# A fused attention and SwiGLU kernel: a POOL chain put first, a centring step one batch later, and Down products spread between Gate and Up pairs

## The chip, the core and the metric

The kernel runs on one core of a Trainium2 chip. The metric is the device time of one execution in microseconds (us). The engines have the profile's names: PE (TensorE, matmul), PEld (its weight loads), DVE (VectorE), ACT (ScalarE), POOL (GpSimd) and SP (SyncE, which only issues DMAs here).

## The reference, cut to what matters

```python
x = A_x                                   # 1 x 2048 x 512, float32
xn = layernorm(x)                         # per token: (x - mean) / sqrt(var + 1e-5)
q, k, v = split(xn @ A_wqkv)              # 32 heads of 16
p = softmax(mask(q @ k.T * 16**-0.5))     # causal, window of 256 keys
s = (p @ v) @ A_wo
h = silu(xn @ B_w1) * (xn @ B_w3)         # Gate and Up: 512 -> 1792
g = silu(h @ B_w2)                        # Down: 1792 -> 512
out = x + s * g
```

## The kernel before, in words

**Tiles.** The 2048 tokens are four tiles `t` of 512, and each tile has four blocks `b` of 128. A float32 product is made from float16 pairs: an operand is cut into a high and a low half, and three matmuls (high·high, high·low, low·high) replace one. So a Gate or an Up product of one 128-wide slice `f` of the 1792 features is 12 matmuls of 128x512 (L1032), issued in two halves of 6. The slices are 0 to 13; `gate_up(t, f)` gives four pieces: Gate's two halves, Up's two halves. PE writes them to one of two PSUM banks, m0 and m1, which every dense product takes in turn (`bank`). ACT then makes tanh of Gate (L1047), DVE multiplies it with Gate's bank (L1051) and later with Up's bank (L1056), and ACT and POOL cut the result into halves (L1065, L339).

**Down products.** For tiles 0 and 1, `down(t, k, b)` multiplies one block of tokens with one group `k` of feature slices: groups are slices 0–3, 4–7, 8–10 and 11–13 (`GROUPS`). With four slices that is 12 matmuls (L1257) in two pieces; DVE takes the bank out (L1278 for the first group, L1281 for the others). Tiles 2 and 3 use a folded form of Down (`folds`, L1175) instead.

**Weights in tile 0.** The Gate, Up and Down weights come in as float32 and are measured and cut beside the other work while tile 0 runs: `measure` (squares on ACT, L249), a short DVE chain for the scale (L294 to L304), and `cut` by `split_pool`: ACT scales (L342), ACT casts the high half (L343), and POOL subtracts for the low half in two pieces of 256 columns (L339). Down's weights go the same way (`measure_down`, L919, L923 to L941). The cut halves are stored to DRAM and only loaded again for the later tiles.

**Token statistics.** `prepare(t)` loads a tile's x, makes mean and variance on DVE (`stats`, L437 and L438), the reciprocal root (`rstd`), and subtracts and scales (`centre`, L475 on DVE). For t > 0 `rstd` starts with three small DVE instructions (L442, L446, L447) and goes on with ten POOL instructions of 128x4 that depend on one another (L463 to L472); their result `rs` is what `centre` waits for. `prepare_beside` puts these steps into a list, and one entry of it is issued with each batch of attention work: for tiles 2 and 3 four `stats`, `rstd`, four `centre`, and then the transposes (`turn_beside`) on PE.

**Order of the work.** Attention work is issued in batches (`batches`, `spread`): score products for the maxima (L661; the maxima on DVE at L675), score products for the softmax (L742; DVE adds the mask, L749; ACT makes the exponential, L752), and the products with V (L770). Between the batches stand the dense pieces in the order of the list that `feed_forward` returns, together with the projections (L593, emptied at L610 and L614) and the V product (L563). A counter goes up by one with each dense piece and each batch; `later(n, f)` runs `f` n steps after now. PE's instructions run in the order in which they are written. The other engines' queues are ordered by a scheduler, by priority; `urgent()` raises the priority of what stands inside. All engines take their queues strictly in order. SBUF tiles of one size ("slots") are given out from a pool of 54 and taken back in order of age.

**The Down list.** In `feed_forward` the variable `late` holds pieces that are appended after the next slice's Gate and Up pieces. When the last slice of a group has been done, all four blocks of `down` go into `late`, and so stand as one lump of up to 48 matmuls behind the next Gate/Up pair.

Of the kernel before, what the change touches and what calls it, by code (L numbers as in the profile page):

```python
# [15 lines left out]
ALU = mybir.AluOpType  # L16
# [18 lines left out]
FB = F // P  # L35
# [4 lines left out]
XS = 2.0**10  # L40
# [14 lines left out]
GROUPS = ((0, 4), (4, 8), (8, 11), (11, 14))  # L55
# [28 lines left out]
def tile_block(ctx: ExitStack, tc: tile.TileContext, x, wqkv, wo, w1, w3, w2, out):  # L84
# [53 lines left out]
    def urgent():  # L138


        return tc.high_priority(offset=200) if started else nullcontext()
# [21 lines left out]
    def bank(shape, dtype=F32):  # L163

        open_bank[0] = b = 1 - open_bank[0]
        return psm.tile(shape, dtype, name=f"m{b}", tag=f"m{b}", bufs=1)
# [258 lines left out]
    def prepare(t):  # L425

        mv = lnpool.tile([P, 4, 2], F32, name="mv")
        rs = lnpool.tile([P, 4], F32, name="rs")
        xts = {}

        def load(b):
            xts[b] = take(F32)
            (nc.scalar if t == 0 and b % 2 else nc.sync).dma_start(xts[b], x[t * TW + b * P:t * TW + (b + 1) * P, :])

        def stats(b):
            st = lnpool.tile([P, nc.vector.BN_STATS_DIM], F32, name="st")
            nc.vector.bn_stats(st, xts[b])  # L437
            nc.vector.bn_aggr(mv[:, b, :], st)  # L438

        def rstd(b0, b1):  # L440
            ve = lnpool.tile([P, b1 - b0], F32, name="ve")
            nc.vector.tensor_scalar(ve, mv[:, b0:b1, 1], 1e-5, None, op0=ALU.add)  # L442


            r0 = lnpool.tile([P, b1 - b0], F32, name="r0")
            nc.vector.tensor_scalar(r0.bitcast(I32), ve.bitcast(I32), 1, None, op0=ALU.logical_shift_right)  # L446
            nc.vector.tensor_scalar(r0.bitcast(I32), r0.bitcast(I32), -1.0, float(0x5F3759DF), op0=ALU.mult, op1=ALU.add)  # L447
            sq = lnpool.tile([P, b1 - b0], F32, name="sq")
            if t == 0:
                nc.vector.tensor_mul(sq, r0, r0)  # L450
                nc.vector.tensor_mul(sq, sq, ve)

                nc.vector.scalar_tensor_tensor(sq, sq, -10 / 3, sq, op0=ALU.add, op1=ALU.mult)
                nc.vector.scalar_tensor_tensor(r0, sq, 5.0, r0, op0=ALU.add, op1=ALU.mult)
                with tc.issue_after(lasts["cast"].ins):
                    nc.vector.tensor_mul(sq, r0, r0)
                nc.vector.scalar_tensor_tensor(sq, sq, -0.5 * (3 / 8)**3 * XS, ve, op0=ALU.mult, op1=ALU.mult)
                nc.vector.scalar_tensor_tensor(rs[:, b0:b1], sq, 1.5 * (3 / 8) * XS, r0, op0=ALU.add, op1=ALU.mult)
                return

            pool = nc.gpsimd
            u = lnpool.tile([P, b1 - b0], F32, name="u")
            pool.tensor_mul(sq, r0, r0)  # L463
            pool.tensor_mul(sq, sq, ve)
            pool.tensor_scalar(u, sq, -10 / 3, None, op0=ALU.add)
            pool.tensor_mul(sq, sq, u)
            pool.tensor_scalar(sq, sq, 5.0, None, op0=ALU.add)
            pool.tensor_mul(r0, r0, sq)
            pool.tensor_mul(sq, r0, r0)
            pool.tensor_mul(sq, sq, ve)  # L470
            pool.tensor_scalar(sq, sq, -0.5 * (3 / 8)**3 * XS, 1.5 * (3 / 8) * XS, op0=ALU.mult, op1=ALU.add)
            pool.tensor_mul(rs[:, b0:b1], sq, r0)  # L472

        def centre(b):
            lasts["centre"] = nc.vector.tensor_scalar(xts[b], xts[b], mv[:, b, 0:1], rs[:, b:b + 1],  # L475
                                                      op0=ALU.subtract, op1=ALU.mult)

        def turn(b):
            if t not in X:
                X[t] = xpool.tile([P, NC, TW], F16, name="XH"), xpool.tile([P, NC, TW], F16, name="XL")  # L480
            xh, xl = X[t]
            c = slice(b * P, (b + 1) * P)

            if b < 2:
                pt = bank([P, NC, P])
            elif b == 2:
                pt = pso.tile([P, 2, TW], F32, name="po")[:, 0, :].rearrange("p (k q) -> p k q", q=P)
            else:
                pt = scores_bank()[:, 0, :].rearrange("p (k q) -> p k q", q=P)
            for k in range(NC):  # L490
                nc.tensor.transpose(pt[:, k, :], xts[b][:, k * P:(k + 1) * P], identf)
            give(xts.pop(b))
            with urgent():
                lasts["xh"] = nc.scalar.copy(xh[:, :, c], pt)

            def rest():
                turned[t] = turned.get(t, 0) + 1
                with urgent():
                    lasts["x"] = nc.vector.tensor_sub(xl[:, :, c], pt, xh[:, :, c])
            later(1, rest)  # L500

        def turn_beside(b, n, s):


            if t not in X:
                X[t] = xpool.tile([P, NC, TW], F16, name="XH"), xpool.tile([P, NC, TW], F16, name="XL")
            xh, xl = X[t]
            for k in range(n, n + 2):
                for h in range(2):
                    for c in range(2):  # L510
                        f = k * P + 64 * c
                        rows = slice(64 * h, 64 * h + 64)
                        nc.tensor.matmul(s[64 * c:64 * c + 64, h, WIN + 64 * (k - n):WIN + 64 * (k - n + 1)],  # L513
                                         xts[b][rows, f:f + 64], identf[rows, rows], start=True, stop=True)
            if n:
                give(xts.pop(b))

            def rest():
                pt = s[:, :, WIN:WIN + P].rearrange("p h (k q) -> p k h q", k=2)
                hi, lo = (a[:, n:n + 2, b * P:(b + 1) * P].rearrange("p k (h q) -> p k h q", h=2) for a in (xh, xl))  # L520
                with urgent():
                    nc.vector.tensor_copy(hi, pt)
                    nc.vector.tensor_sub(lo, pt, hi)
                if n:
                    turned[t] = turned.get(t, 0) + 1
            return rest
        return load, stats, rstd, centre, turn if t == 0 else turn_beside

    def prepare_beside(t, more=0):


        load, stats, rstd, centre, turn = prepare(t)
        made = [(0, lambda b=b: load(b)) for b in range(4)]
        pairs = [(0, 1), (2, 3)] if t == 1 else [(b,) for b in range(4)]
        work = [lambda bs=bs: [stats(b) for b in bs] for bs in pairs]
        work.append(lambda: rstd(0, 4))
        work += [lambda bs=bs: [centre(b) for b in bs] for bs in pairs]
        ready = []

        def turns():  # L540

            ready.append(0)
            if len(ready) == 2:
                besides.extend(lambda s, b=b, n=n: turn(b, n, s) for b in range(4) for n in (0, 2))
        work.append(turns)
        made.append((0, lambda: later(more, lambda: behind.extend(work))))
        return made, turns
# [684 lines left out]
    def folds(t, k):  # L1232

        loads = [(0, lambda kind=kind: load_fold(t, k, kind)) for kind in range(len(KINDS))]
        pieces = []
        for n, i in enumerate(SEVEN):
            pieces += fold_down_piece(t, k, i)
            if n in (0, 2):
                pieces.append(loads[2 + n // 2])
        return loads[:2], pieces  # L1240
# [110 lines left out]
    def feed_forward():  # L1351

        pieces = []
        late = []
        cuts_at = []
        for t in range(NT):
            for f in range(FB):
                if t == 0:
# [8 lines left out]
                    for m in range(f + 1 if f else 0, min(f + 2, FB)):  # L1367
                        k = next(k for k, (_, f1) in enumerate(GROUPS) if m < f1)
                        pieces.append((0, lambda k=k, m=m: later(2, lambda: measure_down(k, m))))
                else:  # L1370
# [7 lines left out]
                    if t == 1 and f in FOLD_AT:  # L1378
                        work = fold_weights(FOLD_AT.index(f))
# [12 lines left out]
                    if t == 1 and f == at:  # L1392
                        made.insert(2, (0, lambda work=work: later(6, work[2])))
                pieces += made
                pieces += late
                late = []
                if t < 2:
                    for k, (f0, f1) in enumerate(GROUPS):
                        if f == f1 - 1:
                            late = [q for b in range(4) for q in down(t, k, b)]  # L1400
                for k, (j0, j1) in enumerate(FOLDS):
                    if t > 1 and f == 2 * j1 - 1:
                        soon, late = folds(t, k)
                        if k == 0 or t == NT - 1:
                            pieces += soon
            if t + 2 < NT:
                pieces.append((0, second))
        return pieces + late


    tiles = [(t, g) for t in range(NT) for g in range(NG)]
# [190 lines left out]
    for n in range(len(units)):  # L1602
        t = n // 8
# [8 lines left out]
        b = n % 8 - (2 if t < 3 else 3)  # L1612
# [6 lines left out]
    for n, u in enumerate(units):  # L1619
# [17 lines left out]
        k = n // 2 + 2  # L1637
# [35 lines left out]
```

## Time and profile before

| | |
|---|---|
| median of 3 runs | 818.14 us (816.59 to 819.52) |
| the profiled execution's own time | 817.82 us |
| its span, first to last instruction | 816.0 us |
| PE busy | 795.2 us, 97% of the span |
| DVE busy | 633.9 us, 78% |
| ACT busy | 392.4 us, 48% |
| POOL busy | 364.0 us, 45% |

The span is 1.82 us shorter than the execution's own time, and that part is not in the trace. A row of the timeline gives the start in us from the span's start, the length of the merged row, the engine, line, operation, tiles and shapes, how many instructions were merged, and in brackets how long the engine was idle just before and whose result ended that. A merged row's length runs from the first start to the last end. PE's matmuls are pipelined: one 128x512 matmul shows about 380 ns, while the next one starts 216 ns after it.

### The profile page before, as it was taken

Reading aid. Unit: us, or ns where it says so; the run is one execution under the profiler, and the core shown is the slowest. Engines: PE = TensorE matmul, PEld = TensorE weight load, DVE = VectorE, ACT = ScalarE, POOL = GpSimd, SP = SyncE. Lnnn points to the kernel's source line nnn. Section 1 sums busy time; section 2 is a strip of 40 time slices with the busy share of each in tenths; the row PEclk is TensorE's granted clock in tenths of the full one; section 3 lists DMA queues with packets and bytes.
Section 4 is the critical chain, followed back from the end, with each engine's and each line's share of the span. In section 5 each row is a group of like instructions: output and inputs, shape, how many; then the busy total and the mean of one; then the engine's idle time right before and its main releaser. Section 6 shows DMA issues by size and latency. Waiting matters only on the chain.

```text
span 816.0 us, 23868 instructions
## 1 busy us (share of the span) xinstructions
PE 795.2 (97%) x9176; PEld 404.2 (50%) x9176; DVE 633.9 (78%) x2037; ACT 392.4 (48%) x591; POOL 364.0 (45%) x648
## 2 busy tenths in 40 slices
PE   8999989998999999999999999999999999999998
PEld 4434444443444444444444544456544654466465
DVE  8788788885898777787988888786777887775437
ACT  6879586563527444444444344434444334344421
POOL 2234266232328636434445264630246377560670
PEclk9999999999999999999999999999999999999999
DMA  9967554735457384666755544646362545325321
GB/s 284 258 218 254 165 179 130 276 115 188 136 141 255 105 267 120 215 180 208 204 169 171 172 100 144 168 128 189 122 197 74 161 127 149 111 77 181 111 56 70
DMA packets 109794, 134.18 MB, mean 164 GB/s; under 512 B 18864, under 2 KB 64880, under 8 KB 109680
## 3 DMA queue, kind: packets, MB, share of 16 engines
q1 hardware_dynamic: 109392, 132.13, 53.9%
q8 instruction: 72, 1.18, 0.6%
q10 hardware_dynamic: 288, 0.52, 0.2%
q14 instruction: 42, 0.34, 0.1%
HBM read 91.23 MB, written 36.57 MB: 157 GB/s over the span
## 4 chain that ended last, share of the span: by engine, by line
PE 78%; DVE 10%; ACT 5%; DMA 3%; issue 3%; SPq 1%; POOL 1%; DVEq 0%; POOLq 0%; ACTq 0%
PE m L1032 29%; PE po L770 8%; PE m L1257 8%; PE m L1175 8%; PE m L593 7%; PE s L742 5%; PE m L1309 4%; PE m L563 4%; PE s L661 3%; DVE junk L675 2%; PE po L661 2%; DMA slot<-in_A_x_dram 1%; DMA dW<-slot 1%; DVE s L749 1%; ACT slot L342 1%
## 5 line engine op out<-in xcount | busy, mean ns | idle before, releaser
L1032 PE MATMUL m<-XH,slot 128*128 128x512 f16 x896 | 267.5, 380 | 1.8 <-DVE slot L614 1.2
L752 ACT ACTIVATE pt<-s,es 128x1024 f32<-128x1024 f32 x152 | 167.6, 1112 | 198.6 <-DVE s L749 183.1
L339 POOL TENSOR_TENSOR slot<-slot,slot 128x256 f16<-128x256 f32 (+1 forms) x170 | 112.9, 691 | 218.2 <-ACT slot L1065 79.2
L1032 PEld LDWEIGHTS <-slot 128*128 128x128 f16 x1344 | 124.8, 98 | 156.2 <-issue 12.7
L1032 PE MATMUL m<-XL,slot 128*128 128x512 f16 x448 | 169.9, 379 | 0.0
L749 DVE TENSOR_TENSOR s<-s,MK 128x256 f32<-128x256 f32 (+2 forms) x280 | 118.7, 434 | 52.7 <-PE s L742 48.5
L675 DVE CUSTOM_DVE_ANT_0 junk<-s,MW 128x320 bf16<-128x320 f32 x276 | 133.9, 485 | 18.0 <-PE s L661 10.3
L675 DVE CUSTOM_DVE_ANT_0 junk<-po,MW 128x320 bf16<-128x320 f32 x172 | 83.4, 485 | 4.3
L1257 PE MATMUL m<-slot,slot 128*128 128x512 f16 x336 | 80.0, 385 | 3.6 <-DVE slot L614 3.2
L770 PE MATMUL po<-pt,V 64*32 64x320 f32 (+4 forms) x2880 | 77.2, 342 | 0.8 <-DVE pp L304 0.8
L593 PE MATMUL m<-XH,slot 128*128 128x512 f16 x240 | 71.0, 380 | 1.5 <-DVE slot L1051 0.8
L1175 PE MATMUL m<-slot,slot 128*128 128x256 f16 x588 | 68.4, 273 | 0.0
L1090 POOL TENSOR_TENSOR slot<-slot,slot 128x256 f16<-128x256 f32 x98 | 64.6, 671 | 1.1
L1047 ACT ACTIVATE slot<-m,sgs 128x512 f32<-128x512 f32 x56 | 38.3, 683 | 54.4 <-PE m L1032 53.1
L770 PEld LDWEIGHTS po<-pt,V 64*32 64x32 f32 x2880 | 50.5, 106 | 22.9 <-PE s L513 0.9
L1175 PEld LDWEIGHTS <-slot 128*128 128x128 f16 x588 | 56.1, 98 | 11.5 <-issue 2.8
L1051 DVE SCALAR_TENSOR_TENSOR slot<-slot,m 128x512 f32<-128x512 f32 x56 | 38.4, 685 | 27.9 <-ACT slot L1047 27.8
L742 PE MATMUL s<-qa,KA 50*64 50x320 f16 (+3 forms) x1472 | 58.6, 260 | 0.3 <-DVE M L675 0.2
L593 PEld LDWEIGHTS <-slot 128*128 128x128 f16 x384 | 35.6, 98 | 44.7 <-issue 3.3
L742 PEld LDWEIGHTS <-KA 50*64 50x64 f16 x1472 | 30.3, 106 | 52.5 <-issue 31.1
L1257 PEld LDWEIGHTS <-slot 128*128 128x128 f16 x336 | 30.9, 98 | 42.7 <-issue 8.9
L661 PE MATMUL s<-KA,qa 48*64 48x320 f16 (+3 forms) x824 | 45.1, 295 | 3.7 <-ACT pt L752 2.9
(188 smaller groups left out, 1095.3 us busy)
## 6 DMA issues: line engine op xcount, KB each, us to landing
slot<-dW SPq DMA_DIRECT2D x98, 256.0 KB
slot<-in_B_w_dram SPq DMA_DIRECT2D x56, 256.0 KB
slot<-dFold SPq DMA_DIRECT2D x48, 256.0 KB
dW<-slot SPq DMA_DIRECT2D x42, 256.0 KB
slot<-in_A_x_dram SPq DMA_DIRECT2D x30, 256.0 KB
KA<-dK SPq DMA_DIRECT2D x24, 288.0 KB
qa<-dQ SPq DMA_DIRECT2D x32, 192.0 KB
slot<-dWQ SPq DMA_DIRECT2D x24, 256.0 KB
```

The source lines that it names most:

```text
L339: op(out[:, c], a[:, c], b[:, c])
L593: nc.tensor.matmul(cell["pp"], w[:, (a * NC + c) * P:(a * NC + c + 1) * P], b[:, c, :], start=(c, i) == parts[0][0], stop=(c, i) == parts[ ...
L661: nc.tensor.matmul(s[c:c + w, r, :n], qa[rows, 2 * p + a, ii * P + c:ii * P + c + w], ka[rows, 2 * p + a, e - n:e], start=True, stop=True)
L675: lasts["maximum"] = nc.vector.tensor_tensor_reduce(out=junk[:, :n], in0=s[:, r, :n], in1=mask, scale=1.0, scalar=NEG, op0=ALU.add, op1=AL ...
L742: nc.tensor.matmul(s[64 * h:64 * h + 64, r, o:o + 64 * n], ka[rows, 2 * p + a, 64 * (m + 4):64 * (m + 5)], qa[rows, 2 * p + a, 64 * (m + k ...
L749: nc.vector.tensor_add(v, v, MK[:, kind, of:of + n, :].unsqueeze(1).to_broadcast([P, 2 * len(which), n, 64]))
L752: lasts["exp"] = nc.scalar.activation(pt, s, AF.Exp, scale=es)
L770: nc.tensor.matmul(cell["po"][32 * i:32 * i + 32, h, 64 * (m + k):64 * (m + k + n)], V[64 * h:64 * h + 64, (4 * t + m // 2) % VB, hd * VW: ...
L1032: nc.tensor.matmul(cell[k], w[:, (a * NC + c) * P:(a * NC + c + 1) * P], b[:, c, :], start=c == 0 and i == 0, stop=c == NC - 1 and i == 2)
L1090: nc.gpsimd.tensor_sub(lo, view, hi)
L1175: nc.tensor.matmul(cell["ps"][:, c], made[:, f:f + P], wj[:, g:g + 256], start=j == j0 and c == 0 and n == 0, stop=j == j1 - 1 and n == 2, ...
L1257: nc.tensor.matmul(ps, hh[:, a * TW + b * P:a * TW + (b + 1) * P], w[:, c * D:(c + 1) * D], start=f == f0 and i == 0, stop=f == f1 - 1 and ...
```

## The change

Three edits. The ten POOL instructions of `rstd` are put inside `urgent()`. For tiles 2 and 3 an empty entry is added to the list after `rstd`, so that `centre` is issued one batch later relative to `rstd` (tile 1 has no such entry). And in `feed_forward`, `late` becomes a list of blocks: while tile 0 runs, one block of Down products is issued after each Gate/Up pair (two after slice 12, all that are left after slice 13) in place of a whole group's four; tiles 1 to 3 issue their blocks as before.

```diff
             pool = nc.gpsimd
             u = lnpool.tile([P, b1 - b0], F32, name="u")
-            pool.tensor_mul(sq, r0, r0)
...
-            pool.tensor_mul(rs[:, b0:b1], sq, r0)
+            with urgent():
+                pool.tensor_mul(sq, r0, r0)
...
+                pool.tensor_mul(rs[:, b0:b1], sq, r0)
...
         work.append(lambda: rstd(0, 4))
+        if t > 1:
+            work.append(lambda: None)
         work += [lambda bs=bs: [centre(b) for b in bs] for bs in pairs]
...
                 pieces += made
-                pieces += late
-                late = []
+                n = len(late) if t or f == FB - 1 or f < GROUPS[0][1] else 2 if f == FB - 2 else 1
+                for work in late[:n]:
+                    pieces += work
+                late = late[n:]
                 if t < 2:
                     for k, (f0, f1) in enumerate(GROUPS):
                         if f == f1 - 1:
-                            late = [q for b in range(4) for q in down(t, k, b)]
+                            late += [down(t, k, b) for b in range(4)]
                 for k, (j0, j1) in enumerate(FOLDS):
                     if t > 1 and f == 2 * j1 - 1:
-                        soon, late = folds(t, k)
+                        soon, work = folds(t, k)
+                        late.append(work)
...
-        return pieces + late
+        return pieces + [q for work in late for q in work]
```

In tile 0 the first group's blocks now stand after slices 4, 5, 6 and 7 and no longer all after slice 4; the second group's after 8 to 11; the third's after slice 12 (two of them) and 13. The Gate/Up pairs of slices 5 to 13 move ahead by as much. PE's order is the same in both kernels before the first moved piece (about 79 us into the span of before) and again from about 190 us on. Line numbers after the edits are higher by 1 in `rstd`'s POOL chain and `centre`, and by 3 further on (L1032 is L1035 after the change, L1257 is L1260).

The first place is POOL's queue at the statistics of tile 2 (r is the first guess of the root, rs the result; on and rb belong to the attention output). Before:

```order
L463 TENSOR_TENSOR sq<-r_3152 128x4
L464 TENSOR_TENSOR sq<-sq,ve 128x4
L465 TENSOR_SCALAR u<-sq 128x4
L466 TENSOR_TENSOR sq<-sq,u 128x4
L339 TENSOR_TENSOR on<-on,rb 128x256 x2
L467 TENSOR_SCALAR sq<-sq 128x4
L841 CAST slot_3259<-on 128x256
L468 TENSOR_TENSOR r_3152<-r_3152,sq 128x4
L841 CAST slot_3259<-on 128x256
L469 TENSOR_TENSOR sq<-r_3152 128x4
L339 TENSOR_TENSOR slot_3259<-on,slot_3259 128x256
L470 TENSOR_TENSOR sq<-sq,ve 128x4
```

After, at the same statistics:

```order
L464 TENSOR_TENSOR sq<-r_3032 128x4
L465 TENSOR_TENSOR sq<-sq,ve 128x4
L466 TENSOR_SCALAR u<-sq 128x4
L467 TENSOR_TENSOR sq<-sq,u 128x4
L468 TENSOR_SCALAR sq<-sq 128x4
L469 TENSOR_TENSOR r_3032<-r_3032,sq 128x4
L470 TENSOR_TENSOR sq<-r_3032 128x4
L471 TENSOR_TENSOR sq<-sq,ve 128x4
L472 TENSOR_SCALAR sq<-sq 128x4
L473 TENSOR_TENSOR rs<-sq,r_3032 128x4
L339 TENSOR_TENSOR on<-on,rb 128x256 x2
```

The chain now stands in one piece, and the 128x256 work on the attention output comes behind it. The chain is also issued 6 steps sooner (step 125, before 131), and its first `centre` 4 steps sooner (131, before 135).

The second place is PE's queue where the second block of Down in tile 0 ends (slot_1129 is the weight of Gate 5, slot_1534 in the changed kernel that of Gate 6). Before, fourth block:

```order
L1257 MATMUL m_1510<-slot_1293,slot_1225 128x512
L1032 LDWEIGHTS slot_1129
L1032 MATMUL m_1547<-XH,slot_1129 128x512
L1032 LDWEIGHTS slot_1129
L1032 MATMUL m_1547<-XH,slot_1129 128x512
```

After, second block, at the same count of PE instructions (rows 1039 to 1043 in both):

```order
L1260 MATMUL m_1539<-slot_1293,slot_1225 128x512
L1035 LDWEIGHTS slot_1534
L1035 MATMUL m_1566<-XH,slot_1534 128x512
L1035 LDWEIGHTS slot_1534
L1035 MATMUL m_1566<-XH,slot_1534 128x512
```

Gate 6 stands where Gate 5 stood. Its weight is cut at the same step as before (step 62 for Gate 6's, 2 steps ahead of its use; before, 11 steps ahead).

The third place is the statistics of tile 1, on POOL and DVE. POOL before (the L339 rows on slots are low halves of weights or of Gate·Up results):

```order
L339 TENSOR_TENSOR slot_1707<-slot_1620,slot_1707 128x256 x2
L463 TENSOR_TENSOR sq<-r_1757 128x4
L464 TENSOR_TENSOR sq<-sq,ve 128x4
L465 TENSOR_SCALAR u<-sq 128x4
L466 TENSOR_TENSOR sq<-sq,u 128x4
L467 TENSOR_SCALAR sq<-sq 128x4
L468 TENSOR_TENSOR r_1757<-r_1757,sq 128x4
```

POOL after (slot_1756 and slot_1827 are the cut Down weights of slices 4 and 5):

```order
L339 TENSOR_TENSOR slot_1756<-slot_990,slot_1756 128x256
L464 TENSOR_TENSOR sq<-r_1807 128x4
L339 TENSOR_TENSOR slot_1756<-slot_990,slot_1756 128x256
L465 TENSOR_TENSOR sq<-sq,ve 128x4
L339 TENSOR_TENSOR slot_1827<-slot_1084,slot_1827 128x256
L466 TENSOR_SCALAR u<-sq 128x4
L339 TENSOR_TENSOR slot_1827<-slot_1084,slot_1827 128x256
L467 TENSOR_TENSOR sq<-sq,u 128x4
L468 TENSOR_SCALAR sq<-sq 128x4
```

DVE from the chain's input r to the first `centre`, before:

```order
L447 TENSOR_SCALAR r_1757<-r_1757 128x4
L882 TENSOR_SCALAR sgs<-pp 128x2
L883 TENSOR_TENSOR p_156<-pp 128x2
L1051 SCALAR_TENSOR_TENSOR slot_1795<-slot_1795,m_1773 128x512
L675 ISA junk,M<-s,MW 128x320
L675 ISA M 128x1
L675 ISA junk,M<-s,MW 128x320
L675 ISA M 128x1
L294 TENSOR_SCALAR al<-s 128x4
L475 TENSOR_SCALAR slot_1492<-slot_1492,mv,rs 128x512
```

DVE after, from the row right behind L447 on (the row of L1054 multiplies with the bank of Gate 7, which is free after it):

```order
L678 ISA junk,M<-s,MW 128x320
L678 ISA M 128x1
L678 ISA junk,M<-s,MW 128x320
L678 ISA M 128x1
L690 TENSOR_SCALAR NM_133<-M 128x16
L476 TENSOR_SCALAR slot_1519<-slot_1519,mv,rs 128x512
L691 SCALAR_TENSOR_TENSOR NM_133<-M,NM_133 128x16
L476 TENSOR_SCALAR slot_1521<-slot_1521,mv,rs 128x512
L788 COPY os<-po 128x512
L789 TENSOR_TENSOR os<-os,po 128x448
L752 TENSOR_TENSOR s<-s,MK 128x4x64
L1054 SCALAR_TENSOR_TENSOR slot_1934<-slot_1934,m_1856 128x512
```

Before, ten small POOL instructions follow one another; after, three 128x256 subtractions stand between the first four of them. On DVE three rows of other work (L882, L883, L1051) have gone from the stretch between L447 and the first `centre`, and `rstd` and `centre` of this tile are issued at the same steps as before (72, 76 and 78).

More of the change, by code (lines that the diff above doesn't have):

```diff
@@ L462, in rstd @@
             u = lnpool.tile([P, b1 - b0], F32, name="u")
[L463 to L472, printed above, removed]
+            with urgent():
+                pool.tensor_mul(sq, r0, r0)
+                pool.tensor_mul(sq, sq, ve)
+                pool.tensor_scalar(u, sq, -10 / 3, None, op0=ALU.add)
+                pool.tensor_mul(sq, sq, u)
+                pool.tensor_scalar(sq, sq, 5.0, None, op0=ALU.add)
+                pool.tensor_mul(r0, r0, sq)
+                pool.tensor_mul(sq, r0, r0)
+                pool.tensor_mul(sq, sq, ve)
+                pool.tensor_scalar(sq, sq, -0.5 * (3 / 8)**3 * XS, 1.5 * (3 / 8) * XS, op0=ALU.mult, op1=ALU.add)
+                pool.tensor_mul(rs[:, b0:b1], sq, r0)
         def centre(b):
```

## Prediction

> **What bounds the kernel now.** I read the page first, then PE's waits, then the timeline around each.
>
> ```profile
> span 816.0 us, 23868 instructions
> PE 795.2 (97%) x9176; PEld 404.2 (50%) x9176; DVE 633.9 (78%) x2037; ACT 392.4 (48%) x591; POOL 364.0 (45%) x648
> ```
>
> PE is busy 795.2 of 816.0 us, and both kernels run the same matmuls. So the change can win at most PE's 20.8 us of idle time, and what a slower clock costs beside it. Next, who made PE wait (time in all, times, longest):
>
> ```profile
> PE m L1257 <- DVE slot L614: 3.2, 1, 3.2
> PE s L661 <- ACT pt L752: 2.9, 3, 1.6
> PE m L1032 <- DVE slot L614: 1.2, 2, 1.0
> ...
> PE m L593 <- DVE slot L1051: 0.8, 1, 0.8
> PE m L593 <- DVE slot L614: 0.7, 1, 0.7
> ```
>
> One wait of 3.2 us stands out; the rest are below 2 us. Here it is, with DVE and POOL, and the windows before, in, and after it (the column behind POOL is the granted clock):
>
> ```profile
> 191.83 1.01 PE L1257 MATMUL m<-slot,slot 128*128 128x512 f16 x2 [3.20 <-DVE slot L614]
> ...
> 190.63 0.55 DVE L475 TENSOR_SCALAR slot<-slot,mv,rs 128x512 f32<-128x512 f32 x1 [3.40 <-POOL rs L472]
> 191.09 0.68 DVE L614 SCALAR_TENSOR_TENSOR slot<-m,slot 128x512 f16<-128x512 f32 x1
> ...
> 184.60 0.20 POOL L463 TENSOR_TENSOR sq<-r 128x4 f32<-128x4 f32 x1 [8.11 <-DVE r L447]
> 185.80 1.42 POOL L339 TENSOR_TENSOR on<-on,rb 128x256 f32<-128x256 f32 x2
> 190.40 0.20 POOL L472 TENSOR_TENSOR rs<-sq,r 128x4 f32<-128x4 f32 x1
> ...
> 184.90:188.20 3.30, 3.30 (x34) 1.58 (x27) 2.04 (x11) 1.60 (x2) 2.85 (x9) 1.00 0.30 88
> 188.70:191.60 2.90, 0.00 (x0) 0.00 (x0) 0.97 (x2) 0.00 (x0) 1.73 (x5) 0.99 0.22 69
> 191.60:194.90 3.30, 3.07 (x16) 1.05 (x19) 0.83 (x2) 0.00 (x0) 0.00 (x0) 0.50 0.67 210
> ```
>
> The chain reads backwards. PE wants a PSUM bank that L614 on DVE must empty. L614 stands behind the first `centre` of tile 2 (L475), and that sits idle for 3.40 us until POOL delivers rs. POOL's chain ran from 184.60 to 190.60, 6.0 us, since six larger instructions stand inside it. Then the clock: PE was still for 2.90 of 2.90 us in the second window, and the third was granted at 0.50. PE was busy there for 3.07 us at half speed, so about 1.5 us of work more was lost. The wait costs 3.2 + 1.5 = 4.7 us.
>
> [...]
>
> **The change part by part.** The sum is made against the profiled execution, 817.82 us (span 816.0 and 1.82 around it); the median of the three runs is 818.14 us, 0.3 us above.
>
> *The chain of tile 2.* Its ten instructions now follow one another. What that takes, tile 1 shows, whose chain was already in one piece:
>
> ```profile
> 104.73 0.20 POOL L463 TENSOR_TENSOR sq<-r 128x4 f32<-128x4 f32 x1 [1.37 <-DVE r L447]
> ...
> 107.31 0.20 POOL L472 TENSOR_TENSOR rs<-sq,r 128x4 f32<-128x4 f32 x1
> ```
>
> 107.51 − 104.73 = 2.8 us in place of 6.0. Also, `centre` is issued 6 steps behind `rstd` and no longer 4. Four dense pieces and a batch lie between, and a piece of 6 matmuls takes 1.3 us (a matmul starts every 216 ns), so rs is there in time. Gain: **−4.7 us**, with ends of −3.2 (the clock falls anyway, for another wait) and −4.7. The attention output's 128x256 instructions go behind the chain, at most 2.8 us later; they feed an output product of a later tile, so I cost that at nothing.
>
> *Tile 3's empty entry.* `centre` goes one batch later, its transposes stay at their steps. Of all waits for rs,
>
> ```profile
>   POOL rs L472: 3.8, 2
> ```
>
> two exist, 3.40 us (tile 2) and the 0.37 us of tile 1 below; tile 3 has none to lose. 0 us; the four `centre` (about 0.6 us each) stay hidden beside PE's matmuls, and would cost 2.4 us at most if none were.
>
> *Gate 6 arrives sooner.* Gate/Up 5 takes the place of Down blocks of the same 24 matmuls, so up to Gate 6 PE's times stay those of before, and Gate 6 starts where Gate 5 did. Its weight is cut at its old step:
>
> ```profile
> 89.82 0.59 PE L1032 MATMUL m<-XH,slot 128*128 128x512 f16 x2
> ...
> 88.68 1.11 ACT L752 ACTIVATE pt<-s,es 128x1024 f32<-128x1024 f32 x1 [8.10 <-PE m L1257]
> 89.69 1.32 ACT L342 ACTIVATE slot<-slot,pi 128x512 f32<-128x512 f32 x2
> 90.92 1.12 ACT L343 CAST slot<-slot 128x512 f16<-128x512 f32 x2
> ...
> 91.60 3.81 POOL L339 TENSOR_TENSOR slot<-slot,slot 128x256 f16<-128x256 f32 x6 [12.01 <-ACT slot L343]
> ```
>
> The high half is there when POOL starts, at 91.60. The second matmul wants the first half of the low part, one of POOL's six: 91.60 + 3.81/6 = 92.24. Unhindered it would start at 89.82 + 0.22 = 90.04. PE loses **+2.2 us**. The ends: 0, if ACT and DVE come to this cut 2 us sooner, and +2.9, if both halves are awaited. The scale comes through DVE's queue, and there the rows ahead of it are the same in kind, so I take 2.2.
>
> *Tile 1's rs.* Here the change may make the wait that it removes from tile 2. The chain now has three halves of L339 between its first rows, and less work on DVE lies between its input (L447) and the first `centre`:
>
> ```profile
> 107.54 0.87 DVE L475 TENSOR_SCALAR slot<-slot,mv,rs 128x512 f32<-128x512 f32 x1 [0.37 <-POOL rs L472]
> ...
> L339 POOL TENSOR_TENSOR slot<-slot,slot 128x256 f16<-128x256 f32 (+1 forms) x170 | 112.9, 691 | 218.2 <-ACT slot L1065 79.2 <-ACT slot L343 64.8 <-DVE slot L1313 50.6
> ...
> L675 DVE CUSTOM_DVE_ANT_0 junk<-s,MW 128x320 bf16<-128x320 f32 x276 | 133.9, 485 | 18.0 <-PE s L661 10.3 <-PE s L285 1.0
> L675 DVE DVE_READ_ACCUMULATOR2_ANT M<- 128x1 f32 x512 | 42.2, 82 | 0.0
> ...
> L687 DVE TENSOR_SCALAR NM<-M 128x16 f16<-128x16 f32 x32 | 9.5, 296 | 0.5
> ```
>
> POOL: 2.8 + 3 x 0.69 = 4.9 us. DVE in that time: two maxima with their reads, 2 x (0.485 + 0.082), and 0.3 for L687, 1.4 us. So DVE would stand still for about 3.5 us. Behind it wait, in DVE's queue, the emptying of the V product, a mask, and L1051 of Gate 7, whose bank the fourth block of Down wants; PE waits with them. Cost: 0 at best (DVE's maxima themselves wait for PE, and cover it), **+3.5** as worked out, +4.7 if the two `centre` of about 0.6 us each, which then stand in front of that bank, are paid too. I take 3.5: PE already waits for DVE hereabouts.
>
> *What the spreading gives back.* In the row above, ACT stood idle for 8.10 us during the lump of Down; afterwards its queue was too full, and PE waited for it and for DVE:
>
> ```profile
> 113.98 0.25 PE L661 MATMUL s<-KA,qa 48*64 48x128 f16 x4 [0.59 <-ACT pt L752]
> ...
> 120.01 0.30 PE L661 MATMUL s<-KA,qa 48*64 48x256 f16 x4 [1.62 <-ACT pt L752]
> ...
> 166.49 0.59 PE L593 MATMUL m<-XH,slot 128*128 128x512 f16 x2 [0.71 <-DVE slot L614]
> ...
> 168.96 0.30 PE L661 MATMUL s<-KA,qa 48*64 48x256 f16 x4 [0.66 <-ACT pt L752]
> ...
> 115.98 1.33 ACT L342 ACTIVATE slot<-slot,sw 128x512 f32<-128x512 f32 x2 [0.86 <-DVE sw L941]
> ...
> 118.87 1.09 ACT L752 ACTIVATE pt<-s,es 128x1024 f32<-128x1024 f32 x1
> ```
>
> At 118.87 the exponential stands behind casts of Down's weights; these are issued eight steps sooner after the change, and the tanh of Gate 5 falls into the idle 8.10 us. I count all four waits as gone, 0.59 + 1.62 + 0.71 + 0.66 = **−3.6 us**; the ends are 0 (they come back elsewhere) and −6, with the waits of 0.8 us and less on DVE in that stretch.
>
> *DMAs.* The loads of the later weights are issued about 8 steps sooner, ahead of the key and query fetch in SP's queue; that fetch is issued here and used at 107.87:
>
> ```profile
> 76.14 0.91 SPq L637 DMA_DIRECT2D KA<-dK  x2
> 78.11 1.04 SPq L864 DMA_DIRECT2D slot<-in_B_w_dram  x2
> ```
>
> Some five issues of about 0.5 us ahead of it leave over 25 us. 0 us. Each slot that is taken in tile 0 was given back at least eight steps before.
>
> **The sum:** −4.7 + 0 + 2.2 + 3.5 − 3.6 = −2.6 us, 817.82 − 2.6 = **815.2 us**.
>
> **The rivals.**
>
> *Tile 1's wait doesn't form* (chance 0.20). If DVE comes to L447 early, its two maxima wait for PE's score products, and the POOL chain runs meanwhile. For it: before, the same place cost only 0.37 us. Against: DVE is 78% busy over the span, and more here. −2.6 − 3.5 = −6.1: 811.7 us.
>
> *Gate 6 doesn't wait* (0.12). ACT gets to the cut sooner, because tanh no longer bunches. Against: the cut starts 1.0 us behind the exponential's start, which itself waits for PE. −2.6 − 2.2 = −4.8: 813.0 us.
>
> *Tile 1's wait halves the clock* (0.21). [...] Price: the 1.5 us measured there, the wait at its upper end of 4.7, and, DVE being late throughout, nothing given back: −4.7 + 2.2 + 4.7 + 1.5 = +3.7, 821.5 us, slower. [...]
>
> *The change doesn't do what it says* (0.05). The POOL queue has work ahead of tile 2's chain, and rs is late all the same: −4.7 falls away, 817.82 + 2.1 = 819.9 us. Against: the chain is issued six steps sooner.
>
> **How the numbers follow.** The forecast's chance is 0.42, and its own range 813.0 to 817.4, as the give-back is worth between about 1.4 and 5.8. About 0.3% (2.5 us) is what a measurement of this kernel can tell from no change, so faster means below 815.4 us, slower above 820.3 us. Faster: 0.53 of the forecast (0.22), nearly all of the first rival (0.19) and of the second (0.11): 0.52. Slower: two thirds of the third (0.14) and a part of the fourth (0.02): 0.16. The rest, 0.32, is the same. The range of 8 in 10 goes from 811.0, a little below the first rival, to 820.5, between the forecast and the third; what lies outside are the lower third of the one and the upper half of the other.
>
> **What would show it.** PE's 3.20 us wait for L614 and the stretch at 0.50 near 191 us are gone, and the POOL chain of tile 2 takes 2.8 us. At about 90 us PE waits some 2 us for ACT and POOL at L1035. At about 110 us DVE waits for rs at L476, and PE shortly after for L1054. PE's waits for the exponential sum to below 1 us. A second stretch at a clock of 0.50, or waits of PE for L1054 and the exponential above 7 us together, would make the forecast wrong.

## The result, and the profile after

The changed kernel takes 819.19 us (median of 22 runs, 818.27 to 820.30) against 818.13 us (22 runs, 816.38 to 819.54): a ratio of 1.0012, with a 95% interval of 1.0006 to 1.0019. The forecast of 815.2 us was wrong in sign. 819.19 us lies outside the forecast's own range (813.0 to 817.4) and inside the wider one of 8 in 10 (811.0 to 820.5), whose upper end lies between the forecast and a rival's 821.5. The profiled execution took 819.83 us, 2.0 us more than that of before, and its span is 2.0 us longer too:

```profile
span 818.0 us, 23873 instructions
...
PE 796.7 (97%) x9176; PEld 404.5 (49%) x9176; DVE 636.1 (78%) x2037; ACT 393.4 (48%) x591; POOL 364.1 (45%) x648
```

Of these 2.0 us PE's busy time makes 1.5 (796.7 − 795.2, for the same matmuls) and its idle time 0.5 (818.0 − 796.7 = 21.3, against 20.8).

**Tile 2's wait is gone.** POOL's chain and the first centring step (the timeline of POOL, then of DVE, after):

```profile
184.03 0.20 POOL L464 TENSOR_TENSOR sq<-r 128x4 f32<-128x4 f32 x1 [7.18 <-DVE r L447]
...
186.61 0.20 POOL L473 TENSOR_TENSOR rs<-sq,r 128x4 f32<-128x4 f32 x1
...
190.28 0.54 DVE L476 TENSOR_SCALAR slot<-slot,mv,rs 128x512 f32<-128x512 f32 x1
```

The chain takes 186.81 − 184.03 = 2.8 us in place of 6.0, L476 shows no wait in brackets, and PE has none near 191 us.

**Gate 6 waits, as expected.** PE at that place, after:

```profile
89.20 0.81 PE L1260 MATMUL m<-slot,slot 128*128 128x512 f16 x3
91.62 0.39 PE L1035 MATMUL m<-XH,slot 128*128 128x512 f16 x1 [1.61 <-ACT slot L343]
92.37 0.39 PE L1035 MATMUL m<-XH,slot 128*128 128x512 f16 x1 [0.36 <-POOL slot L339]
```

1.61 us for the cast of the high half, and 0.36 us for POOL's first low half.

**Tile 1 waits, as expected.** POOL, DVE and PE, after:

```profile
111.25 0.20 POOL L464 TENSOR_TENSOR sq<-r 128x4 f32<-128x4 f32 x1
111.40 0.67 POOL L339 TENSOR_TENSOR slot<-slot,slot 128x256 f16<-128x256 f32 x1
...
115.35 0.20 POOL L473 TENSOR_TENSOR rs<-sq,r 128x4 f32<-128x4 f32 x1
...
115.59 0.86 DVE L476 TENSOR_SCALAR slot<-slot,mv,rs 128x512 f32<-128x512 f32 x1 [3.48 <-POOL rs L473]
...
119.39 0.68 DVE L1054 SCALAR_TENSOR_TENSOR slot<-slot,m 128x512 f32<-128x512 f32 x1
...
120.12 2.24 PE L1260 MATMUL m<-slot,slot 128*128 128x512 f16 x6 [3.85 <-DVE slot L1054]
```

Read it backwards: PE waits 3.85 us for a bank that L1054 empties; L1054 stands six rows behind L476; L476 waits 3.48 us for rs. With three subtractions inside, POOL's chain takes 115.55 − 111.25 = 4.3 us.

**Two stretches at half clock in place of one.** The two stretches at 0.50, each of 3.41 us, and as long a window ahead of each (the columns are start:end, length, the busy time and count of PE, PEld, DVE, ACT and POOL, the granted clock, DMA share and GB/s):

```profile
89.93:93.34 3.41, 1.44 (x7) 0.50 (x6) 0.85 (x3) 3.41 (x7) 1.70 (x3) 1.00 0.52 136
93.34:96.75 3.41, 3.41 (x31) 1.40 (x30) 2.31 (x13) 2.13 (x3) 3.38 (x6) 0.50 0.34 84
117.23:120.64 3.41, 0.52 (x3) 0.28 (x3) 3.34 (x9) 0.27 (x1) 1.18 (x2) 1.00 0.04 13
120.65:124.06 3.41, 3.41 (x27) 1.21 (x26) 2.81 (x13) 1.58 (x3) 1.00 (x2) 0.50 0.38 112
```

The clock is 0.50 from 93.34 to 96.76 and from 120.64 to 124.06 us. Two 128x512 matmuls of L1035 take 96.76 − 95.91 = 0.85 us there, from the first one's start to that of the next behind them, and 97.41 − 96.97 = 0.44 us after it, so I estimate that each stretch costs up to 3.41 / 2 = 1.7 us. PE is busy 1.5 us longer than before with one such stretch more, so I count about 1.5 us for each. The second was a rival's; the first, behind a wait of 2.0 us in all, I had not expected.

**The waits for the exponential went, and others came.** PE's waits from 94 to 190 us, after (total, times, longest):

```profile
PE m L1260 <- DVE slot L1054: 4.2, 2, 3.8
PE m L1035 <- DVE slot L1059: 1.3, 1, 1.3
PE po L773 <- DVE XL L524: 1.1, 1, 1.1
PE s L285 <- DVE sb L926: 0.9, 1, 0.9
PE po L773 <- DVE M L678: 0.7, 1, 0.7
PE po L664 <- DVE XL L524: 0.2, 1, 0.2
```

Without tile 1's wait these are 4.2 − 3.85 + 1.3 + 1.1 + 0.9 + 0.7 + 0.2 = 4.6 us, against 6.4 us in the same stretch of before (whose list is that of the first experiment below, but for 0.1 us). All of them are for DVE.

### The profile page after: what moved, and what is told of

Same layout as the page of the kernel before. It is cut to its first block, busy times and chain, and to the rows that moved or that the text cites. A ratio compares the mean times of both kernels' runs of the same rounds, so it can differ in the third digit from the quotient of the medians.

```text
span 818.0 us, 23873 instructions
## 1 busy us (share of the span) xinstructions
PE 796.7 (97%) x9176; PEld 404.5 (49%) x9176; DVE 636.1 (78%) x2037; ACT 393.4 (48%) x591; POOL 364.1 (45%) x648
## 4 chain that ended last, share of the span: by engine, by line
PE 79%; DVE 11%; issue 4%; ACT 4%; DMA 1%; POOL 1%; DVEq 0%; ACTq 0%; POOLq 0%
PE m L1035 30%; PE po L773 9%; PE m L596 8%; PE m L1178 8%; PE m L1260 7%; PE s L745 5%; PE m L1312 4%; PE m L566 4%; DVE junk L678 3%; PE s L664 3%; PE po L664 2%; DVE s L752 1%; DVE slot L1054 1%; ACT slot L342 1%; ACT sqa L249 1%
## 5 line engine op out<-in xcount | busy, mean ns | idle before, releaser
L1035 PE MATMUL m<-XH,slot 128*128 128x512 f16 x896 | 268.4, 381 | 4.7 <-ACT slot L343 1.6
L339 POOL TENSOR_TENSOR slot<-slot,slot 128x256 f16<-128x256 f32 (+1 forms) x170 | 113.5, 696 | 215.7 <-ACT slot L1068 78.0
L1035 PEld LDWEIGHTS <-slot 128*128 128x128 f16 x1344 | 124.8, 98 | 160.4 <-issue 14.2
L1035 PE MATMUL m<-XL,slot 128*128 128x512 f16 x448 | 170.2, 380 | 0.0
L1260 PE MATMUL m<-slot,slot 128*128 128x512 f16 x336 | 79.9, 384 | 4.6 <-DVE slot L1054 4.6
L1054 DVE SCALAR_TENSOR_TENSOR slot<-slot,m 128x512 f32<-128x512 f32 x56 | 38.4, 685 | 29.6 <-ACT slot L1050 29.5
L1260 PEld LDWEIGHTS <-slot 128*128 128x128 f16 x336 | 31.1, 98 | 44.1 <-issue 10.0
L1059 DVE SCALAR_TENSOR_TENSOR slot<-m,slot 128x512 f32<-128x512 f32 x56 | 38.5, 687 | 10.9 <-PE m L1035 10.7
```

The costliest lines, as they stand in the source:

```text
L339: op(out[:, c], a[:, c], b[:, c])
L1035: nc.tensor.matmul(cell[k], w[:, (a * NC + c) * P:(a * NC + c + 1) * P], b[:, c, :], start=c == 0 and i == 0, stop=c == NC - 1 and i == 2)
L1054: lasts["emptied"] = nc.vector.scalar_tensor_tensor(sg, sg, 1.0, cell[0], op0=ALU.add, op1=ALU.mult)
L1260: nc.tensor.matmul(ps, hh[:, a * TW + b * P:a * TW + (b + 1) * P], w[:, c * D:(c + 1) * D], start=f == f0 and i == 0, stop=f == f1 - 1 and ...
```

## The experiments

The theory behind them: tile 2's wait was worth what the forecast said, and the spreading costs it again at Gate 6 and at tile 1, by the two waits and by the half clock that they bring. The rivals: the first two edits do nothing by themselves, or the spreading itself costs through DVE, whatever becomes of the two waits.

### The first two edits without the spreading

The changed kernel with the Down list of before:

```diff
-                n = len(late) if t or f == FB - 1 or f < GROUPS[0][1] else 2 if f == FB - 2 else 1
...
+                pieces += late
+                late = []
...
-                            late += [down(t, k, b) for b in range(4)]
+                            late = [q for b in range(4) for q in down(t, k, b)]
```

> The kernel before with the first two edits alone (the POOL chain urgent, the empty entry for tiles 2 and 3); Down stands in lumps as before. Theory: the wait of 3.20 us near 191 us and the half-clock stretch behind it go, and nothing else moves, so 4.7 us less than before: about 813.4 us, one stretch of 0.50 less (none left), PE's waits for the exponential still 2.9 us in all. Rival 1: these two edits do nothing without the spreading, since the POOL chain of tile 2 is still issued late with the attention output's work in it: 818.1 us and the wait still there. Rival 2: the wait goes, but a later one of the same slack takes its place: 815 to 817 us.

Measured: 813.31 us (6 runs, 813.20 to 814.25), ratio to before 0.9943 (0.9929 to 0.9956). The theory's number. But not by a shorter chain (POOL, then DVE):

```profile
184.64 0.20 POOL L464 TENSOR_TENSOR sq<-r 128x4 f32<-128x4 f32 x1 [8.10 <-DVE r L447]
...
190.46 0.20 POOL L473 TENSOR_TENSOR rs<-sq,r 128x4 f32<-128x4 f32 x1
...
193.20 0.54 DVE L476 TENSOR_SCALAR slot<-slot,mv,rs 128x512 f32<-128x512 f32 x1
```

The chain still takes 6.0 us; the centring step simply comes 2.5 us after its end. PE's waits from 94 to 190 us here, which are those of before:

```profile
PE s L664 <- ACT pt L755: 2.9, 3, 1.6
PE po L773 <- DVE pp L304: 0.8, 1, 0.8
PE m L596 <- DVE slot L1054: 0.8, 1, 0.8
PE m L596 <- DVE slot L617: 0.7, 1, 0.7
PE po L664 <- DVE XL L524: 0.6, 1, 0.6
PE s L664 <- DVE al L295: 0.3, 1, 0.3
PE s L745 <- DVE M L678: 0.2, 1, 0.2
PE m L1035 <- DVE slot L617: 0.2, 1, 0.2
```

### The spreading without the first two edits

```diff
-            with urgent():
-                pool.tensor_mul(sq, r0, r0)
+            pool.tensor_mul(sq, r0, r0)
...
-        if t > 1:
-            work.append(lambda: None)
```

> The changed kernel without its first two edits: Down spread in tile 0, no urgent chain, no empty entry. Theory: all that the change lost is in the first 170 us and comes of the spreading, so Gate 6's wait (about 2 us), tile 1's wait for rs (about 3.9 us) and a half-clock stretch behind each stay, and with them tile 2's wait of 3.2 us and its stretch may return: between 819.2 us (as the changed kernel) if tile 2's chain, issued six steps sooner, is in time without the two edits, and 823.9 us if it isn't. Rival: the loss comes of the urgent chain or the empty entry, and spreading alone gives about 815 us.

Measured: 818.61 us (12 runs, 817.87 to 819.97), ratio 1.0012 (1.0002 to 1.0022). The loss comes of the spreading, as the theory had it; the rival's 815 us is out. Tile 2's wait of PE does not return: POOL's chain starts 1.1 us sooner than before, the first work on the attention output comes only at 189.72 us (185.80 before), and so the chain takes 2.8 us without being urgent (183.47 to 186.26 us); L475 waits 0.98 us for rs, and PE not at all. So the spreading had removed that wait already, and in the whole change the first two edits add nothing to it. Tile 1's wait (3.35 us) and Gate 6's (1.62 and 0.36) are there.

### Gate 6's weight cut earlier

```diff
-... later(5, lambda: measure(f, 1)) if f == 6 else measure(f, 1)))
+... later(1, lambda: measure(f, 1)) if f == 6 else measure(f, 1)))
```

> The changed kernel with the measure of slices 6 and 7 issued four steps sooner, so that Gate 6's weight is cut 7 steps ahead of its use and no longer 2. Theory: PE's waits of 1.6 and 0.4 us at Gate 6 go, and with them the half-clock stretch at 93 us (3.4 us at half speed, 1.6 us): 819.2 - 2.0 - 1.6 = 815.6 us, and one stretch of 0.50 instead of two. Rival 1: the stretch at 93 us comes of something else than this wait; then only 2.0 us go: 817.2 us. Rival 2: ACT and POOL have that work to do in any case, and PE waits as long elsewhere: 819.2 us.

Measured: 817.43 us (12 runs, 815.57 to 818.76), ratio 0.9987 (0.9975 to 0.9999). That is rival 1's number: 1.8 us less than the changed kernel. In the trace both waits at Gate 6 are gone, and with them the stretch behind them, but there are two stretches at 0.50 all the same, one of them at 78.84 us, behind other waits (its rows stand below). One of these the early cut brings itself: PE waits 0.74 us for the exponential at 77.03 us. So the number alone doesn't say that the stretch at 93 us had another cause; the next run and the one with the filler bear on that.

### Tile 1's centring step one batch later

```diff
-        if t > 1:
+        if t:
             work.append(lambda: None)
```

> The changed kernel with the empty entry for tile 1 too, so that its first centring step stands two steps later, behind the copies of the attention output, a mask and the row L1054 that frees PE's bank. Theory: the wait of 3.85 us for L1054 at 120 us and the half-clock stretch behind it go: 819.2 - 3.8 - 1.6 = 813.8 us. Rival 1: only the stretch goes, as DVE is late there anyway and PE waits 2 to 3 us all the same: 816 to 817.5 us. Rival 2: the centring steps, two steps later, hold up the transposes and projections of tile 1 by as much as they saved: 819 us or more.

Measured: 814.41 us (7 runs, 814.07 to 816.54), ratio 0.9959 (0.9945 to 0.9973), near the theory's 813.8 us. DVE and PE at that place:

```profile
116.41 0.69 DVE L1054 SCALAR_TENSOR_TENSOR slot<-slot,m 128x512 f32<-128x512 f32 x1 [1.96 <-ACT slot L1050]
...
117.15 1.02 PE L1260 MATMUL m<-slot,slot 128*128 128x512 f16 x4 [0.52 <-DVE slot L1054]
```

L1054 now waits for ACT and no longer behind rs, and PE waits 0.52 us for it instead of 3.85. Gate 6's two waits are still there (1.62 and 0.36 us). By their mean granted clock five of the seven runs have no stretch at 0.50 (0.999 to 1.000) and two have one (0.997); the profiled execution, the slowest, is one of these two, and its stretch starts at 93.83 us, right behind Gate 6's waits.

### The urgent chain alone, and the empty entry alone

Each of the first two edits by itself, on the kernel before:

> The kernel before with the first edit alone: the POOL chain urgent. With both of the first edits the chain of tile 2 still took 6.0 us with the same six larger instructions inside (184.64 to 190.66 us), and the first centring step stood at 193.20, behind it. Theory: so the urgent chain does nothing, and the empty entry did all of it: 818.1 us, the wait of 3.2 us and the stretch at 0.50 still there. Rival: the urgent chain counts too, 814 to 816 us.

Measured: 817.53 us (12 runs, 815.89 to 819.94), ratio 0.9997 (0.9985 to 1.0009): nothing. POOL's chain still has the larger instructions inside and takes 6.0 us (184.50 to 190.49 us). PE's wait is still there too, but the profiled execution, whose span is 1.5 us shorter than that of before, has no stretch at 0.50 behind it. The window that holds the wait, and the one behind it:

```profile
188.30:191.70 3.40, 0.23 (x2) 0.00 (x0) 1.18 (x3) 0.00 (x0) 2.02 (x6) 1.00 0.24 60
191.70:195.10 3.40, 3.38 (x31) 1.53 (x31) 2.14 (x8) 0.45 (x1) 0.00 (x0) 1.00 0.78 202
```

And PE's wait, from the timeline:

```profile
191.72 0.59 PE L1258 MATMUL m<-slot,slot 128*128 128x512 f16 x2 [3.19 <-DVE slot L615]
```

Behind the same wait, 3.19 us here and 3.20 before, the clock stayed at 1.00 in one execution and was 0.50 in the other; on what that hangs, no run shows.

> The kernel before with the second edit alone: the empty entry for tiles 2 and 3. Theory: it takes the whole wait of tile 2: 813.3 us, as the two edits together. Rival: the chain must be urgent too: 815 us or more.

Measured: 813.06 us (6 runs, 812.97 to 813.59), ratio 0.9939 (0.9926 to 0.9952). The empty entry alone does all that the two edits do.

### Both cures

> The changed kernel with both cures, Gate 6's measure four steps sooner and the empty entry for tile 1 too. Theory: the two losses are separate and add up: 819.2 - 1.8 - 4.8 = 812.6 us, and no stretch at 0.50 in most runs; so spreading Down is worth 0.7 us by itself against the first two edits alone (813.3 us). Rival 1: spreading gives nothing back, 813.3 us. Rival 2: the two are the same lost time twice, 814.4 us.

Measured: 812.62 us (6 runs, 812.18 to 812.87), ratio 0.9932 (0.9919 to 0.9946), with a granted clock of 1.000 in every run. The losses at Gate 6 and tile 1 are separate and add up. This is the fastest kernel here, ahead of both the kernel before and the changed one. PE's waits from 94 to 190 us:

```profile
PE s L285 <- DVE sb L926: 1.3, 1, 1.3
PE m L1035 <- DVE slot L1059: 1.3, 1, 1.3
PE po L773 <- DVE XL L524: 1.3, 1, 1.3
PE m L1260 <- DVE slot L1054: 0.9, 2, 0.5
PE po L773 <- DVE M L678: 0.7, 1, 0.7
PE po L664 <- DVE XL L524: 0.2, 1, 0.2
```

5.7 us here against 6.5 us with the lumps, 0.8 us less in this list; the times differ by 0.7 us (813.31 − 812.62). But the early cut brings its wait of 0.74 us for the exponential at 77.05 us here too, and over the whole span PE stands still 16.8 us in both traces (811.5 − 794.7 with the lumps, 810.8 − 794.0 here). So in these two traces the 0.7 us do not come from PE's waits, and what the spreading is worth by itself stays open.

### PE kept busy while Gate 6's weight is awaited

```diff
+                if (t, f, k) == (0, 6, 0):
+                    for _ in range(8):
+                        nc.tensor.matmul(cell[k].rearrange("p (a q) -> p a q", a=4), onesb,
+                                         onesb.unsqueeze(1).to_broadcast([P, 4, P]), start=True, stop=True)
```

> The changed kernel with eight matmuls of ones that nobody reads, 128x512 each, written into Gate 6's bank right ahead of Gate 6, so that PE is busy for about 1.7 us while it would wait for the weight; the wait for the weight itself stays. [...]

The forecast: if PE's standing still at Gate 6 brings the stretch at 93 us, a mean clock of 0.997 to 0.998 in all runs, that of one stretch, and a median of 818.8 us; if it doesn't, runs with one and with two stretches as after the change, and 819.2 to 819.5 us.

Measured: 818.76 us (12 runs, 816.75 to 819.98), ratio 1.0009 (0.9998 to 1.0021). PE at Gate 6:

```profile
90.11 1.89 PE L1035 MATMUL m<-onesb 128*128 128x512 bf16 x8
91.89 0.39 PE L1039 MATMUL m<-XH,slot 128*128 128x512 f16 x1
92.64 0.39 PE L1039 MATMUL m<-XH,slot 128*128 128x512 f16 x1 [0.36 <-POOL slot L339]
```

The weight is awaited as long as before, but PE stands still for 0.36 us only, and in this trace the clock stays at 1.00 there (in both windows of 88.84 to 92.25 and 92.25 to 95.66 us). The median is that of the first case, but not all runs have one stretch: by their mean clock eight of twelve do (0.997 to 0.998), three have two (0.996), one has none (1.000). Eleven of 22 runs of the changed kernel had two (0.995 to 0.996); with so few runs, three of twelve against eleven of 22 supports the first case but doesn't prove it, and the runs with two stretches, as the second case has them, stayed in part.

## Why the prediction was wrong, step by step

| Term | Forecast, us | Measured, us |
|---|---|---|
| tile 2's wait with its half clock | −4.7 | −4.7 in the profiles; −4.9 for the empty entry alone |
| tile 3's empty entry | 0 | no wait for it in the profile |
| Gate 6's wait | +2.2 | +2.0 (1.61 + 0.36); 1.8 back when it is cured |
| tile 1's wait | +3.5 | +3.85; 4.8 back, clock included, when it is cured |
| given back by the spreading | −3.6 | −1.8 (4.6 − 6.4); with both cures the times are 0.7 lower than with the lumps |
| half clock behind the new waits | 0 | +3.0 in the profiles (two of about 1.5) |
| sum | −2.6 | +2.35 by these terms; the spans differ by +2.0 |

The 0.35 us over lie mostly in the first 20 us, where PE's order is the same in both kernels: it stands still there for 2.91 us after the change and for 3.26 us before. The medians differ by 1.06 us only: the profiled execution of after is one of the eleven runs with two stretches (mean clock 0.995), and that of before has one (0.998).

**Right:** Gate 6 and tile 1 in place, cause and size; tile 2's gain in place and size; PE's waits for the exponential did go.

**The step that failed first, the half clock.** The forecast took the 1.5 us away with tile 2's wait and charged nothing for the waits that it put in its place, although it made tile 1's longer than the one wait that had halved the clock. It kept that for a rival (0.21, 821.5 us), and for Gate 6's 2.0 us it was in no case at all. Both came in the profiled execution, and a second stretch was what the forecast itself had named as the sign of being wrong. This alone turns −2.6 into +0.4. Over the runs it is less: by the mean clock none, one and two stretches are about equally frequent before (16, 16 and 15 of 47, the table at the end), and after, all 22 runs have one or two (11 and 11). So the clock that the forecast counted as won was not won: such stretches became somewhat more frequent. From what length on a wait is followed by one, no run shows: behind 1.61 and 0.36 us at Gate 6 the clock was 0.50 after the change, behind 3.19 us with the urgent chain alone it was 1.00.

**The second step, the give-back, wrong in size.** All four waits that were counted as gone went, and the smaller ones beside them, but waits for DVE of 0.7 to 1.3 us came instead. Why DVE is later there (it is 78% busy) I read only from the order of its queue; no run takes it apart. The forecast had "they come back elsewhere" as the end of its range and should have stood nearer to it.

**Right number, wrong credit.** The forecast gave tile 2's gain to the chain in one piece, and to the later `centre`. The runs show three things: urgency alone does nothing (817.53), the empty entry alone does everything, with the chain at 6.0 us (813.06), and the spreading alone removes the wait too, by a chain that starts sooner and takes 2.8 us (818.61, no such wait). Two of the three edits reach the same gain of 4.7 us, and one of these two brought two new losses of 1.8 and 4.8 us by the cures. Without the spreading the change would have been worth 4.8 us.

## What to carry to other kernels

A gain that several edits reach is to be had once: ask of each edit alone what it adds, above all of the one that moves the most work. When an edit trades one idle time of PE for another, the price of the half clock, here about 1.5 us for a stretch, belongs on both sides. And work that is spread ahead of its old place makes the next thing early: check that its weight is cut, and its statistics are done, a few steps ahead.

## What the runs showed of the clock

Where the half clock comes differs between executions, and the length of PE's wait alone doesn't tell it. These stretches at 0.50 stand in the traces while PE has work, each with the time for which PE stood still in the 3.41 us ahead of it:

| Kernel | 0.50 from, us | PE still in the 3.41 us ahead, us |
|---|---|---|
| before | 191.56 | 2.93 |
| changed | 93.34 | 1.97 |
| changed | 120.64 | 2.89 |
| spreading alone | 10.72 | 1.80 |
| spreading alone | 119.95 | 3.03 |
| early cut | 78.84 | 1.65 |
| early cut | 119.80 | 2.59 |
| tile 1's entry | 93.83 | 1.92 |
| filler | 119.56 | 3.12 |

The rows for the smallest two of these that aren't at Gate 6, the first ones of the spreading alone and of the early cut:

```profile
7.31:10.72 3.41, 1.61 (x11) 0.65 (x9) 3.10 (x20) 1.76 (x5) 0.00 (x0) 1.00 1.10 341
10.72:14.13 3.41, 3.41 (x18) 3.07 (x17) 2.81 (x6) 2.01 (x4) 0.00 (x0) 0.50 1.13 301
75.43:78.84 3.41, 1.76 (x27) 0.72 (x26) 3.41 (x11) 3.41 (x8) 0.74 (x3) 1.00 1.01 258
78.84:82.25 3.41, 3.41 (x10) 1.22 (x9) 3.31 (x16) 2.79 (x7) 1.25 (x2) 0.50 1.01 346
```

And three places where the clock stays at 1.00, of the early cut, of the kernel before, and Gate 6 of the spreading alone:

```profile
7.16:10.57 3.41, 1.70 (x11) 0.72 (x10) 3.10 (x20) 1.79 (x5) 0.00 (x0) 1.00 1.10 349
10.57:13.98 3.41, 2.83 (x22) 2.03 (x20) 3.12 (x7) 3.04 (x6) 0.00 (x0) 1.00 1.13 284
116.47:119.88 3.41, 1.80 (x16) 0.75 (x16) 2.53 (x13) 3.41 (x8) 1.99 (x4) 1.00 0.62 194
119.88:123.29 3.41, 3.28 (x52) 1.91 (x52) 2.62 (x12) 3.41 (x8) 2.08 (x4) 1.00 0.02 5
89.23:92.64 3.41, 1.85 (x9) 0.65 (x7) 2.59 (x12) 3.06 (x6) 1.30 (x2) 1.00 0.17 39
92.64:96.05 3.41, 2.99 (x34) 1.34 (x35) 0.95 (x5) 2.80 (x7) 3.33 (x6) 1.00 0.85 194
```

So 1.65 us of standing still are followed by a stretch in one trace, and 3.41 − 1.70 = 1.71 us in the same trace are not. Gate 6's waits of 1.61 and 0.36 us are followed by one after the change; its 1.62 and 0.36 us with the spreading alone are not, and neither are the 3.19 us of the urgent chain alone, though the 3.20 us of before are. What decides it, no run shows.

In the runs the stretches show as levels of the mean granted clock, one stretch being, by estimate, 3.41 x 0.5 / 816 = 0.002 of it:

| Kernel | clock 0.999 to 1.000 | 0.997 to 0.998 | 0.994 to 0.996 |
|---|---|---|---|
| before (47 runs, beside the experiments) | 16 | 16 | 15 |
| changed (22) | 0 | 11 | 11 |
| spreading alone (12) | 0 | 8 | 4 |
| both cures (6) | 6 | 0 | 0 |

The first two levels of before have their middle at about 816.6 and 818.0 us: the spread between its runs is mostly tile 2's wait, and whether a stretch at 0.50 follows it: with that wait gone, by the empty entry alone or with both of the first two edits, 10 of 12 runs are in the first level and none in the third. No trace shows where the second stretch of the third level lies. One run with the filler and two with the early cut show no stretch (mean clock 1.000), though tile 1's wait is 3.86 us in the profiled executions of these two kernels; the three runs themselves have no trace.
